# Fused attention and Fourier gate on one core: pair-wise loads of q and k, folded transforms, a new order

## The chip, the core and the metric

The kernel runs on one core of a Trainium2 chip. The metric is the device time of one execution, in microseconds; the lower, the better. The engines are PE (matrix products; PEld is its weight load), DVE (VectorE), ACT (ScalarE), POOL (GpSimd, here mostly the queue that issues casting loads) and SP (SyncE, the queue of the other transfers).

## The reference

Four batches, 8 heads, 768 tokens, head width 64, model width 512. Attention with a window of 96 tokens and 8 global tokens, a linear bias per head, then a gate with a circular convolution over the tokens, done by Fourier transform:

```python
scores = scale * q @ k.T + bias          # bias = -slope[h] * distance, masked outside window and globals
a = softmax(scores); x = a @ v           # x: (B, S, H*D)
x1, x2, x3 = split(x @ w_proj)           # 512 columns each
x2 = irfft(rfft(x2) * rfft(filter))      # over the 768 tokens
out = (x1 * x2 * x3) @ w_out
```

## The kernel before

Everything is 16-bit in SBUF with 32-bit sums. A batch passes two stages; the next batch's attention is interleaved with the present batch's convolution.

**Attention.** k and v are cut into 7 tiles of 120 tokens with the 8 global tokens in front (`GRP` groups the tiles: 0-1, 2-3, 4-6); q into 6 tiles of 128 tokens. `load_q`, `load_run` and `load_rows` load a tile with all 8 heads, k and v over POOL's queue with a cast, q of batch 0 as 32-bit over SP into the output buffers `ot`. `turned` (and `turned32` for batch 0's q) transposes a tile by products with the identity (L640, L627) into `QT` and `KT`. `scores` makes, for a head pair and a group, the products of k and q with 64 rows, two heads side by side (L680). In batch 0 the bias is added by products of `slope` (diagonals) with the distance tile `near`, in two halves of 64 rows (L671), and in the later batches by a product with `mask` on DVE (L711). ACT takes the exponential (L694). `values` (L729, L734) sums with v, which has columns of ones for the denominators; DVE divides (L753); `transpose_x` gives `xT`.

**Gate and convolution.** `gate` makes x1 and x3 (L843) and their product `g`. `butterfly` splits x over the 768 tokens by a factor of 6 on DVE (sums and differences of L788 to L799: `xo`, `xr`, `xcf`). `conv` projects these (L910), `spectra` transforms them by products with the cosine and sine tables `fwd` (L614): two products of 512 columns for each of four outputs, one for each of two. DVE multiplies by the filter's spectrum (`h1`, `h2`; `prod`, `sums`). The inverse (L935, L938) has per bank two products of 256 columns and two of 128. `mixed` and `gated` undo the factor of 6 and multiply by the gate on DVE (L1018 to L1041); the last product with `wo` (L962) is evacuated into `ot` and stored over SP.

**Setup.** `setup`, `load_first`, `distances`, `masks` and `tables` fill constants: ones columns of both v buffers (L1097, L1099), `near`, `slope`, `mask`, the tables (an angle product on PE, rounding on DVE, a sine on ACT; here behind the exponentials of batch 0), then `spectrum` transforms the filter. Before any data is there, PE runs filler products on zeros (L302, the words `i26b1` and the like in the order).

**Order.** The order of all 1025 steps is written out in `ORDER`, with the engine and the PSUM banks of each: `97P01` is step 97 on PE with banks 0 and 1, `98A` step 98 on ACT. Each engine runs its steps in that order; many evacuations may be on ACT or DVE, and the word says which. The steps are numbered as the code makes them.

Of the kernel before, what the change touches and what calls it, by code (L numbers as in the profile page):

```python
# [16 lines left out]
P = 128  # L17
# [3 lines left out]
MAGIC = 12582912.0  # L21
H_SCALE = 1.0 / 32.0
# [17 lines left out]
0V 8V 31V 11V 7V 12V 1V 10V 9V 17S 50S 15S 16S 48S 49S 58S 18G 5G 39A 35A 42A 43A 45A 41A 6A 47A 37A 32A 2A  # L40
38A 36A 33A 46A 51A 19G 22G 23V 28A 40A 44A 26V 55G 24G 71V 72A 77A 34A 79A 52V 25V 61G 54G 59G 60G i26b1 80P0
86P1 87V 81V 29V 259G 20G 21G 57G 67G 56G 62G 3G i2b3 89P2 90V 27V 30V 88V 53V 13V 261S 260G 64G 63G 65G 257G
256G 258G 68G 66G 70G 69G 82P3 83A 84P4 85A 74A i3b1 109P5 110A 75A 115P3 116V i1b0 91P67 92A 93P01 94A 113P2
114V 269G 270G 267G 268G 273G 263G 95P45 96A 78A 161P6 111P7 112V 157P3 158V 162V 14V 97P01 98A 119P45 120A
123P23 124A 121P67 122A 159P0 160V 262S 265S 264S 275G 274G 276G 279G 277G 266G 271G 155P1 156V 104P45 105V
106V 4V 117P23 118A 167P01 168A 165P67 166A 163P45 164A 99P23 100V 101V 215P0 216A 76A 107P1 108V 130P67 131V
132V 125P23 126V 127V 217V 218V 169P45 170A 73A 102P1 103A 220P6 360P7 488G 490S 272G 495G 133P2 134A 219A
221A 128P3 129V 176P45 177V 178V 361V 171P01 172V 150P3 152V 173V 222V 223V 140P2 142A 356P4 357A 179P5 180V
135P7 358P3 359A 224A 137A 174P2 175V 209V 226V 201V 202V 151P4 153A 154V 204V 371P01 365P23 366A 372A 145P5
147V 208V 203V 210V 211V 205V 206V 196P4 227P6 232A 146P7 148A 149V 234V 230V 235V 212V 207V 213V 236V 237V  # L50
225V 373V 214V 136P5 138A 198A 182P2 192P3 194A 368P01 369A 362P45 363A 197P7 199A 191P3 141P0 143A 228A 231A
193A 229A 233A 144V 238V 370V 195V 298P1 285P0 286A 281P7 282A 184A 386P6 387A 299A 498G 499G 294P0 295A 384P7
385V 239V 367V 139V 283P3 284A 186P6 188A 394P45 395A 397P01 398A 430P7 431V 289P2 290V 364V 181P3 309P6 310A
183A 432P7 433V 240V 396V 503G 504G 278G 489G 492G 485G 486G 502G 497G 487G 388P45 389A 391P01 392A 434P2 435V
390V 491S 505G 501G 496G 187P6 189A 296P7 297A 379P45 380V 381V 436P23 437A 374P01 375V 399V 376V 393V 720G
247P6 248A 439P45 440A 441V 438V 307P7 308A 287P2 288A 241P3 442P01 443A 405P45 406V 190V 407V 242V 382P6 383A
243P7 244A 302P2 303A 400P01 401V 402V 377P6 378V 444V 445P45 446A 447V 408P7 245P3 246A 300P2 301A 249P01
251A 409A 250V 403P6 404A 253P45 254A 255A 304V 292V 448P23 449V 450A 185V 453P01 454V 291V 455V 293V 252V
200V 311V 312V 722S 493S 729G 426P7 420P6 421P4 415P5 417A 422A 423A 411P0 413A 410P1 584P5 585A 456P6 457V
305V 660P4 661A 588P0 589V 306V 717G 713G 735G 716G 718S 494S 714G 313P2 314A 317P3 451P5 452A 412A 318A 479V  # L60
478V 425P6 614P2 615A 727G 734G 506G 726G 280G 732G 662P0 719S 721S 464P4 466A 428A 427A 586P1 587V 414V 612P5
613V 481V 480V 725G 508G 724G 658P3 730G 500G 715G 728G 731G 733G 723G 507G 736G 321P2 322A 663A 323P4 324A
327P1 328V 429V 482V 659V 424V 483V 474P7 476A 319P2 320A 469P0 471A 599P45 600A 590P67 591A 325P2 315P1 316A
326A 473P0 475V 484V 329V 330V 331V 522P3 523A 625P45 596P67 597A 598V 622P01 623A 624V 468P2 526P3 527A 470A
626A 509P6 510V 592V 332V 333V 524P7 525A 616P01 593P23 594A 617A 511P6 512V 601V 595V 336V 513P7 514A 664P45
665A 619P23 667P01 668A 620A 458P6 460V 477V 337V 459P7 461A 517P4 416P5 418A 518A 607P01 602P23 603V 608V
419V 604V 609V 621V 618V 334V 666V 335V 627V 515P7 516A 535P5 536A 530P6 531A 350P4 351A 537P5 812P7 813A
353P6 354A 673P23 674A 538A 670P01 671A 463P4 465A 528P7 529A 842P6 843V 628P23 629V 462V 630V 675V 672V 344P5
610P6 611A 345A 816P4 890P7 605P2 606A 817A 633P01 634V 635V 669V 520V 539V 519V 533V 472V 347P6 348A 631P5
886P3 636P2 637A 887A 632A 891A 341P4 676P01 677V 814P6 815A 342A 681P23 682V 540V 678V 532V 683V 467V 534V  # L70
521V 840P5 841A 644P7 888P6 889A 646A 648P4 650A 653P5 655A 679P0 680A 643P1 645V 847P67 848A 821P45 822A
684P2 547P0 548V 685V 823V 706V 849V 707V 649P3 651A 555P6 556A 549P7 550A 853P01 827P45 828A 898P23 899A
545P6 546A 854A 338P7 339V 708V 340S 349S 352S 355S 346S 343S 638P4 640A 551P5 552A 541P2 553P3 554V 709V 710V
711V 543P6 544A 542A 557V 558V 712V 559V 702P7 818P01 819A 850P45 851A 687P6 639P3 641A 689A 642V 900V 820V
560V 652V 561V 564V 754P2 755A 704A 741P4 742A 844P01 845A 846V 829V 824P23 825A 826V 565V 562V 901P67 902A
739P5 740A 737P4 738A 750P0 892P23 895P67 896A 893A 751A 686P1 688A 752P5 692P4 694A 753A 763P2 743P3 765P0
766A 835P67 836V 837V 563V 903V 697P4 654P1 656A 764A 767V 894V 852V 897V 745P0 746A 699A 744A 578P5 758P1
756P2 757A 759A 856P67 857V 647V 855V 696P4 698A 566P3 567A 579A 568S 580S 830P01 831V 832A 858V 768V 747V
691P4 693A 909P23 910V 761V 581P5 582A 861P67 862V 863A 911V 748V 904P01 905V 749V 906V 760V 575P4 701P2 833P3
834V 657V 912P5 859P6 860A 913A 569P7 838P0 839V 762V 703V 864P6 865A 570A 571S 583S 907P1 908A 934V 935V 936V  # L80
937V 695V 938V 939V 940V 773P3 572P5 573A 774A 769P0 781P6 775P1 777P5 783P7 784A 776A 771P2 772A 782A 778A
770A 867P3 872P7 874A 869A 779P2 780A 785V 786V 700V 787V 788V 690V 789V 790V 791V 792V 958P1 954P0 955A 576A
959A 577S 574S 945P5 946A 941P3 942A 915P0 943P2 944A 969P6 970A 956P1 957A 947P7 948A 882P3 949P2 950A 917A
951V 919P4 967P1 968V 952V 971V 953V 972V 962P5 960P2 961A 884A 877P6 871P7 873A 963A 965V 964V 705V 966V 793V
876P2 866P3 868A 879A 870V 881P7 986P5 990P3 973P0 974A 991A 987A 794P6 977P1 978A 979P0 980V 988P3 989A 975P5
976A 883A 981V 875V 885V 982V 929P1 992P3 993A 878A 795A 994V 995V 983V 984V 996V 997V 985V 796S 800P5 801A
797P0 798A 799S 802S 914P7 916A 918V 999V 998V 880V 1001V 1002V 1000V 803P5 804A 805S 925P6 809P7 810A 811S
920P5 922A 931A 806P0 807A 927A 921A 1014V 1012V 923V 1013V 808S 924P5 926A 928V 1006P7 1007A 1008S 930P6 932A
933V 1015V 1009P4 1010A 1011S 1003P5 1004V 1005S 1022P4 1023V 1024S 1016P7 1017V 1018S 1019P6 1020A 1021S
"""  # L90

# [1135 lines left out]
```

## Time and profile before

| | |
|---|---|
| median of 3 runs | 174.79 us (174.55 to 174.84) |
| profiled execution, first to last instruction | 172.9 us (the profile gives no other time of this execution) |
| busy: PE, DVE, ACT, POOL | 166.8, 158.4, 151.9, 75.8 us |
| weight loads | 106.1 us |
| instructions: PE, DVE, ACT, POOL | 1732, 352, 305, 97 |
| moved by DMA | 20.74 MB |
| granted PE clock | 1.000 |

A row of a group of instructions reads: line, engine, operation, out<-in with shapes, count | busy us, mean ns of one | idle time of the engine ahead of them and who ended it. "Busy" is time in which at least one instruction of the engine is in flight; instructions overlap, so the start-to-start distance is shorter than the mean. A row of the chain of waits is start, length, engine, tile, line, count. A row of the table of stretches is the stretch, its length, busy time (instructions) of PE, PEld, DVE, ACT and POOL, granted clock, DMA share and GB/s. Start times are in us from the first instruction.

### The profile page before, as it was taken

Reading aid. Unit: us, or ns where it says so; the run is one execution under the profiler, and the core shown is the slowest. Engines: PE = TensorE matmul, PEld = TensorE weight load, DVE = VectorE, ACT = ScalarE, POOL = GpSimd, SP = SyncE. Lnnn points to the kernel's source line nnn. Section 1 sums busy time; section 2 is a strip of 40 time slices with the busy share of each in tenths; the row PEclk is TensorE's granted clock in tenths of the full one; section 3 lists DMA queues with packets and bytes.
Section 4 is the critical chain, followed back from the end, with each engine's and each line's share of the span. In section 5 each row is a group of like instructions: output and inputs, shape, how many; then the busy total and the mean of one; then the engine's idle time right before and its main releaser. Section 6 shows DMA issues by size and latency. Waiting matters only on the chain.

```text
span 172.9 us, 4486 instructions
## 1 busy us (share of the span) xinstructions
PE 166.8 (96%) x1732; PEld 106.1 (61%) x1732; DVE 158.4 (92%) x352; ACT 151.9 (88%) x305; POOL 75.8 (44%) x97
## 2 busy tenths in 40 slices
PE   7998999999999999999999999999999999999990
PEld 2374988655665668764657867645577755574530
DVE  6869969999999999999999999999989999989970
ACT  2999899999999999999999999999797897678821
POOL 7999998629989964999760000000000000000000
PEclk9999999999999999999999999999999999999999
DMA  4999999999999996999999000720030303003554
GB/s 86 188 198 166 168 171 177 207 184 153 154 161 145 153 148 50 126 147 175 152 151 57 4 0 4 272 91 0 4 121 6 121 2 121 4 0 151 213 205 161
DMA packets 91133, 20.74 MB, mean 120 GB/s; under 512 B 83864, under 2 KB 88040, under 8 KB 91112
## 3 DMA queue, kind: packets, MB, share of 16 engines
q0 software_dynamic: 80912, 12.14, 96.6%
q1 hardware_dynamic: 10200, 8.31, 15.3%
q8 instruction: 13, 0.21, 0.5%
q14 instruction: 8, 0.07, 0.1%
HBM read 25.84 MB, written 6.29 MB: 186 GB/s over the span
## 4 chain that ended last, share of the span: by engine, by line
PE 93%; DVE 4%; issue 0%; ACT 0%; ACTq 0%; DVEq 0%
PE bank L843 25%; PE bank L910 12%; PE bank L962 12%; PE bank L614 6%; PE bank L680 6%; PE bank L640 6%; PE bank L935 5%; PE bank L302 5%; PE bank L729 4%; PE bank L774 4%; PE bank L734 3%; PE bank L671 2%; PE bank L938 1%; DVE KT L306 1%; DVE vn L1097 1%; DVE vn L306 1%
## 5 line engine op out<-in xcount | busy, mean ns | idle before, releaser
L843 PE MATMUL bank<-xT,w 128*128 128x384 f16 x256 | 48.7, 326 | 0.0
L694 ACT ACTIVATE E<-bank 128x864 f16<-128x864 f32 x48 | 40.6, 902 | 1.3 <-PE bank L680 1.3
L843 PEld LDWEIGHTS <-w 128*128 128x128 f16 x256 | 23.4, 98 | 15.6 <-issue 0.7
L322 POOL DMA_DIRECT2D kn<-in_k_dram x28 | 25.7, 921 | 10.7 <-PE bank L640 4.3
L322 POOL DMA_DIRECT2D vn<-in_v_dram x28 | 25.6, 921 | 1.7 <-DMA wo<-in_moe_w_out_dram 1.1
L962 PE MATMUL bank<-wo,y 128*128 128x512 f16 x96 | 23.8, 379 | 0.0
L711 DVE TENSOR_TENSOR E<-E,mask 128x864 f16<-128x864 f16 x36 | 20.6, 600 | 0.0
L322 POOL DMA_DIRECT2D qn<-in_q_dram x18 | 16.3, 918 | 0.3 <-issue 0.2
L753 DVE TENSOR_TENSOR xn<-bank,rc 128x512 f16<-128x512 f32 (+1 forms) x21 | 16.1, 771 | 0.3
L853 ACT CAST g<-bank 128x384 f16<-128x384 f32 x32 | 15.4, 512 | 1.1 <-PE bank L843 0.9
L310 ACT ACTIVATE ot<-bank 128x512 f32<-128x512 f32 x20 | 11.9, 611 | 4.9 <-PE bank L962 4.9
L729 PE MATMUL bank<-vn,E 128*128 128x65 f16 x224 | 15.2, 193 | 0.0
L729 PEld LDWEIGHTS <-E 128*128 128x128 f16 x224 | 14.0, 97 | 1.8
L734 PE MATMUL bank<-vn,E 128*128 128x65 f16 x192 | 14.9, 193 | 0.0
L306 ACT CAST eo<-bank 128x384 f16<-128x384 f32 x28 | 12.7, 512 | 1.7 <-PE bank L938 0.9
L680 PE MATMUL bank<-QT,KT 64*128 64x216 f16 (+2 forms) x224 | 14.0, 241 | 0.0
L306 ACT CAST X<-bank 128x512 f16<-128x512 f32 x22 | 12.7, 613 | 1.3 <-PE bank L614 1.2
L962 PEld LDWEIGHTS <-y 128*128 128x128 f16 x96 | 8.8, 98 | 8.1
L310 ACT ACTIVATE ab<-bank 128x512 f16<-128x512 f32 x22 | 12.8, 619 | 1.1 <-PE bank L910 1.0
L310 ACT ACTIVATE x<-bank 128x384 f16<-128x384 f32 x26 | 13.1, 523 | 0.8 <-ACT g L853 0.4
L734 PEld LDWEIGHTS <-E 128*128 128x128 f16 x192 | 13.1, 97 | 0.7
L680 PEld LDWEIGHTS <-KT 64*128 64x128 f16 x224 | 8.5, 94 | 6.6 <-issue 5.0
(144 smaller groups left out, 369.3 us busy)
## 6 DMA issues: line engine op xcount, KB each, us to landing
out_dram<-ot SPq DMA_DIRECT2D x24, 256.0 KB
kn<-in_k_dram POOLq DMA_DIRECT2D x28, 120.0 KB, 6.3
vn<-in_v_dram POOLq DMA_DIRECT2D x28, 120.0 KB, 6.4
qn<-in_q_dram POOLq DMA_DIRECT2D x18, 128.0 KB, 6.5
ot<-in_q_dram SPq DMA_DIRECT2D x6, 256.0 KB
w<-in_moe_w_proj_dram POOLq DMA_DIRECT2D x4, 256.0 KB, 7.3
g<-in_moe_filter_fft_dram POOLq DMA_DIRECT2D x1, 768.0 KB, 11.0
w<-in_moe_w_proj_dram POOLq DMA_DIRECT2D x1, 512.0 KB, 12.7
```

Source lines behind the costliest of these rows:

```text
L306: {"A": nc.scalar.copy, "V": nc.vector.tensor_copy, "G": nc.gpsimd.tensor_copy}[e](out, in_)
L310: self.nc.scalar.mul(out, in_, c)
L322: return self.g.op(eng, 0.57 + 0.00035 * nbytes[0] if eng == "G" else 0.5, lambda _: e.dma_start(dst, src), w=w, r=r, nbytes=nbytes, name= ...
L680: nc.tensor.matmul(bs[hh].f32()[:, off:off + w], self.KT[hs, hp, P * m:P * m + P], self.QT[hs, hp, KL * m:KL * m + w], start=(off == 0 and ...
L694: g.op("A", act(864), lambda _: nc.scalar.activation(eo, bs[0].two()[:, :, 0:432].rearrange("p h (m w) -> p h m w", m=2), Act.Exp, scale=s ...
L711: g.op("V", dve(864, 2), lambda _: nc.vector.tensor_mul(eo, eo, mk), r=[("mask", 2 * hp), ("mask", 2 * hp + 1)], w=[("E", hp, gi)], name=" ...
L729: nc.tensor.matmul(o[:, n, hh], ef[:, at:at + P], vt[:, t, 2 * hp + hh, 0:D + 1], start=first, stop=(t == 0), skip_group_check=True)
L734: nc.tensor.matmul(o[:, n, hh], ef[:, at:at + P], vt[:, t - 1, 2 * hp + hh, 0:D + 1], start=False, stop=True, skip_group_check=True)
L753: nc.vector.tensor_mul(to, o[:, :, :, 0:D], rc.to_broadcast([P, 2, 2 * nt, D]))
L843: nc.tensor.matmul(bk.f32()[:, 0:h], self.w[:, c, o + P * j:o + P * j + P], self.xT[:, c, h * s:h * s + h], start=(c == 0), stop=(c == 3))
L910: nc.tensor.matmul(bk.f32(), src[:, c], w[:, c, DM:2 * DM], start=(c == 0), stop=(c == 3))
L962: nc.tensor.matmul(bk.f32(), y[:, c, P * t:P * t + P], self.wo[:, c, :], start=(c == 0), stop=(c == 3))
```

## The change

- **q and k by head pair.** `load_pair` loads, for a head pair, all 768 tokens of q and k in six 128-token tiles: two loads for q, two for k, over POOL; for pair 0 of batch 0 over SP as 32-bit into `stage` (the space of `h1`, `h2`) with a cast by DVE or ACT. `turned` makes 6 transposes for a pair's q or k; k's evacuation puts the 120-token tiles and the global tokens together in three pieces. The global rows of k are no longer copied by SP.
- **Tables first.** `tables` moves ahead of the attention and has a third bank of angles (`fold`, half-shifted); the warming ACT function is the sine. The filter's load is at the head of POOL's loads.
- **Biases.** `dg` holds one distance tile with all 128 rows and 648 columns; a block is two products of 128 rows and 432 columns.
- **Folded transforms.** `butterfly` adds and subtracts mirrored halves (`xs`), so that `spectra` needs one product for each of four outputs; `mixed` undoes the fold behind the inverse (`uw`), whose products have 128 columns. Three of these four kinds of adds have an operand or result with a step of minus one.
- **Lighter fills.** The ones are written as pairs in 32-bit words and fewer of them; `kn` needs no zeros; the global rows of v are copied by SP.
- **New order.** 1034 steps, 14 filler products in place of 32, evacuations redistributed; the last batch's last output tile is stored in two halves.

```diff
-        self.qn = t("qn", [P, 6, H, D])
-        self.kn = t("kn", [P, 7, H, D])
+        self.qn = t("qn", [P, 4, 6, 2, D])
+        self.kn = t("kn", [P, 4, 6, 2, D])
...
+    def load_pair(self, b, hp):
+        for i, (what, x, dst) in enumerate((("q", self.q, self.qn), ("k", self.k, self.kn))):
+            to = dst[:, hp]
+            if b or hp not in self.PLAIN:
+                for hh in range(2):
+                    self.load("G", to[:, :, hh], x[b, 2 * hp + hh].rearrange("(t p) d -> p t d", p=P),
+                              [(what + "n", hp, hh)], (768, 256), f"{what}{hp}")
+                continue
...
+            for t in range(6):
+                nc.tensor.transpose(b.f16()[:, P * t:P * t + P], buf[:, hp, t].rearrange("p h d -> p (h d)"), self.ident)
...
+            self.copy(e, kt[:, 0:6, NG:], src[:, 0:6 * KL].rearrange("p (t c) -> p t c", t=6))
+            self.copy(e, kt[:, 6, NG:], src[:, S - KL:S])
+            self.copy(e, kt[:, :, 0:NG], src[:, None, 0:NG].to_broadcast([P, 7, NG]))
...
-                for at, w in runs:
-                    for k in range(2):
-                        for hh in range(2):
-                            hs = slice(64 * hh, 64 * hh + 64)
-                            nc.tensor.matmul(bs[hh].f32()[:, off:off + w], self.slope[hs, hp, k],
-                                             self.near[hs, k, at:at + w], start=(off == 0 and k == 0),
-                                             stop=False, skip_group_check=True)
+                for hh in range(2):
+                    o = bs[hh].f32()[:, 0:432]
+                    nc.tensor.matmul(o if gi != 1 else o.rearrange("p (a b) -> p a b", a=2),
+                                     self.slope[:, 2 * hp + hh], at, start=True, stop=False, skip_group_check=True)
...
+        right, left = cf[:, :, :, 64:P], cf[:, :, :, 63::-1]
+        turned = xs.rearrange("p (a b) c m -> p a b c m", a=2)[:, ::-1, :, :, 64:P]
+        def odd(_):
+            for a in range(2):
+                ins = slice(2 * a, 2 * a + 2)
+                v.tensor_sub(turned[:, a], right[:, ins], left[:, ins])
+        op(dve(512 * n, 2), lambda _: v.tensor_add(xs[:, :, :, 0:64], right, left), ("xr", "xc", "xf"), "xe")
+        op(2 * dve(256 * n, 2), odd, ("xr", "xc", "xf"), "xd")
...
-            self.forward((s,), lambda i, t: self.ab[i][:, t], lambda i, t: [("ab", i, t)], [bk])
+            g.op("P", pe(512), lambda _, bk=bk, i=i, t=t, table=table: nc.tensor.matmul(
+                bk.f32(), table, self.ab[i][:, t], start=True, stop=True), acq=[bk], name="fwd",
+                r=[("ab", i, t), ("fwd", 1 if s > 3 else 3)])
...
-                            nc.tensor.matmul(o[:, 0:P] if z else o[:, P:3 * P], X[:, s, cs],
+                            to = o[:, 0:P] if z else o[:, P:3 * P].rearrange("p (a m) -> p a m", m=64)
+                            to = to if z else to[:, 1:3] if s % 2 else to[:, 0:4:3]
+                            nc.tensor.matmul(to, X[:, s, cs],
                                              self.inr[:, s - 4] if z else self.inv[:, (s + 2) % 4],
...
+        op(lambda _: v.tensor_add(both[:, :, :, 64:P], even, odd), (), "up")
+        op(lambda _: v.tensor_sub(both[:, :, :, 63::-1], even, odd), (), "um")
...
+            self.nc.vector.memset(vt[:, 0, :, self.D:].bitcast(F32), ONES)
+            self.nc.vector.memset(vt[:, 1:, :, self.D:self.D + 2].bitcast(F32), ONES)
...
+        self.load("S", vt[0:NG, 2:7], vt[0:NG, 0:1].to_broadcast([NG, 5, self.H, self.VD]), [("vng", 0, 1)],
+                  (40, 16 * self.VD), "vglobal", r=[("vng", 0, 0, 0), ("vn1", 0)])
```

572 lines of the change are left out of this document (242 added, 330 removed).

## The prediction

> **What bounds the kernel now.** First the busy times and the chain of waits on the page, then the table of stretches.
>
> ```profile
> PE 166.8 (96%) x1732; PEld 106.1 (61%) x1732; DVE 158.4 (92%) x352; ACT 151.9 (88%) x305; POOL 75.8 (44%) x97
> PE 93%; DVE 4%; issue 0%; ACT 0%; ACTq 0%; DVEq 0%
> 0.00:30.00 30.00, 28.32 (x377) 19.31 (x378) 23.75 (x65) 25.37 (x50) 27.83 (x44) 1.00 1.76 165
> 30.00:120.00 90.00, 90.00 (x963) 57.91 (x962) 88.93 (x189) 88.82 (x168) 48.00 (x54) 1.00 1.44 122
> 120.00:165.00 45.00, 45.00 (x380) 27.53 (x379) 42.99 (x97) 36.49 (x88) 0.00 (x0) 1.00 0.19 71
> 165.00:172.90 7.90, 3.46 (x17) 1.37 (x14) 2.68 (x5) 1.20 (x2) 0.00 (x0) 1.00 0.52 200
> ```
>
> Read quickly, this says "PE": 96% busy, 93% of the chain. The stretches (columns after the length: PE, PEld, DVE, ACT, POOL) say more. From 30 to 120 us three engines are full at once: DVE is idle for 1.07 of 90 us, ACT for 1.18. Only from 120 to 165 is PE alone: ACT idles 8.5 us, DVE 2.0. So taking work from PE pays at once in the last third; in the middle, DVE and ACT take its place as the limit. DVE's idle time is 6.25 us up to 30, 3.1 up to 165, and then 0.6 until its last instruction; what follows that is the tail.
>
> Durations overlap, so a sum needs start-to-start distances:
>
> ```profile
> 66.12 0.89 PE bank L640 x16
> 137.39 1.30 PE bank L843 x8
> 138.69 0.27 PE bank L935 x3
> 164.14 4.33 PE bank L962 x20
> 158.38 0.42 DVE L1021 TENSOR_TENSOR eo<-mix,eo 128x512 f16<-128x512 f16 x1
> 158.72 0.42 DVE L1022 TENSOR_TENSOR eo<-mix,eo 128x512 f16<-128x512 f16 x1
> 156.51 1.58 ACT L310 ACTIVATE ot<-bank 128x512 f32<-128x512 f32 x3
> 167.63 0.69 DVE L312 TENSOR_SCALAR ot<-bank 128x512 f32<-128x512 f32 x1 [0.17 <-PE bank L962]
> ```
>
> PE: 0.0556 us for 128 columns, 0.1625 for 384, 0.2165 for 512. The three of L935 are two of 256 and one of 128, so (0.27 - 0.056)/2 = 0.107 for 256. DVE: two of 512 start 0.34 apart and last 0.42, so an instruction that follows directly costs its duration less 0.08. ACT: (1.58 less one duration of about 0.61)/2 = 0.49 for 512. DVE ends at 167.63 + 0.69 = 168.3, 4.6 before the end: that tail (last evacuation and store) I keep, since the new order also ends with a whole 512-column product, evacuation and store.
>
> **What PE loses.**
>
> ```profile
> L935 PE MATMUL bank<-inv,X 128*128 128x256 f16 x64 | 11.3, 273 | 0.0
> L614 PE MATMUL bank<-ab,fwd 128*128 128x512 f16 x40 | 11.3, 379 | 0.0
> L640 PE MATMUL bank<-ident,kn 128*128 128x128 f16 x112 | 8.9, 219 | 0.4 <-DVE KT L306 0.4
> L640 PE MATMUL bank<-ident,qn 128*128 128x128 f16 x72 | 5.7, 219 | 0.0
> 10.63 1.04 PE L627 MATMUL bank<-p,ot 128*128 128x128 f32 x8
> 17.86 0.37 PE bank L671 x8
> ```
>
> Folded inverse: 64 products go from 256 to 128 columns, 64 x 0.051 = -3.3. Folded forward: 40 products become 24 (one, not two, for each of four outputs), 16 x 0.2165 = -3.5. Transposes: 184 at 0.0556 and 24 of 32 bits at (1.04 - 0.27)/7 = 0.11 are 12.9 us; 192 at 0.0556 are 10.7: -2.2. Biases: eight 64-row products of 216 columns take 0.37 a block, since the two halves run side by side; two of 128 rows and 432 columns, between 0.1625 and 0.2165, take 0.36: nothing. The third angle bank adds 0.4. PE in all: -8.6 us.
>
> **What DVE gains and loses.**
>
> ```profile
> L795 DVE TENSOR_TENSOR xo<-xab,xcf 128x1024 f16<-128x1024 f16 x3 | 2.1, 687 | 0.0
> L753 DVE TENSOR_TENSOR xn<-bank,rc 128x512 f16<-128x512 f32 x14 | 9.5, 685 | 0.3
> L1097 DVE MEMSET vn<- 128x1792 f16 x1 | 1.6, 1552 | 0.3 <-issue 0.3
> L306 DVE COPY vn<-vn 8x2560 f16<-8x2560 f16 x1 | 1.5, 1467 | 0.0
> L397 DVE MEMSET kn<- 8x1280 uint32 x1 | 1.1, 1125 | 0.2 <-issue 0.2
> L306 DVE COPY eo<-dg 64x264 bf16<-64x264 bf16 x3 | 1.4, 459 | 0.0
> L306 DVE COPY eo<-dg 64x216 bf16<-64x216 bf16 x3 | 1.1, 352 | 0.1
> L306 DVE CAST eo<-bank 128x384 f16<-128x384 f32 x4 | 2.2, 552 | 0.0
> L306 DVE CAST X<-bank 128x512 f16<-128x512 f32 x2 | 1.4, 682 | 0.0
> ```
>
> Folding moves half of the transform's adds to DVE. With L795 less the overlap, 1024 elements cost 0.61; 512 cost 0.34; so a fixed part of 0.07. Before the transform a batch gets one add of 1024 and two of 512 (1.29 us; batch 0, in halves, 1.5), behind it two of 1024 (1.21; the last batch, in halves, 1.36): 5.4 + 5.0 = +10.4. That holds if a reversed operand keeps the rate; no row shows one. The far bound is L753's one element a cycle: 1024 elements then take 0.61 + 0.53. Three such thousands a batch have a reversed operand, so at most 12 x 0.53 = +6.4 more. I take nothing, since the nearest rows (16-bit, in SBUF, steps of one) are L795's. The Trainium skill, "VectorE: DVE Perf Modes", section "Mode 2×_1P — pack two bf16 into one 32-bit read", asks for 16-bit types and a step of plus or minus one; by that rule too the sum gets nothing, and no run here shows a step of minus one.
>
> Further: two casts of q and k for the first pair, two more rounding steps of the third angle bank, and the constant columns: about +2.5, by L795's and L753's rates. Away go the two memsets of ones (L1097 and its like for the second buffer, 2 x 1.47, for lighter ones that I put at 0.4 each: -2.1), the copy of the global rows (-1.4, to SyncE's queue), the fill of kn (-1.05), the six copies of dg (3 x 0.38 + 3 x 0.27 = -1.95), and about ten small ones that I put at -1.8 together. The order moves casts: counted in the two orders, DVE keeps none of its 4 eo and 2 X and one fewer of ab and x1, and two fewer of ot: 4 x 0.47 + 2 x 0.6 + about 2.3 = -5.4. ACT gets these at about 0.4 to 0.49 each (+4) and loses some slope, near and table-load time, so it stays about level. The evacuations of q and k change shape (21 by DVE before; 10 of 768 and 7 in three pieces after; both 9.4): nothing. DVE in all: +10.4 + 2.5 - 8.3 - 5.4 = -0.8.
>
> So PE gets 8.6 us of air, while DVE keeps 158.4 - 0.8 = 157.6. DVE becomes the bound, and its idle time decides.
>
> **Idle time at the start.**
>
> ```profile
> 29.18 1.30 PE bank L843 x8
> 20.30 0.06 PE bank L729 x2
> L322 POOL DMA_DIRECT2D kn<-in_k_dram x28 | 25.7, 921 | 10.7 <-PE bank L640 4.3 <-PE bank L843 3.2 <-DMA w<-in_moe_w_proj_dram 1.3
> L322 POOL DMA_DIRECT2D g<-in_moe_filter_fft_dram x1 | 0.8, 832 | 0.0
> DMA to landing us min/median/max: 5.2/6.6/12.7
> 17.10 0.56 POOL L380 IOTA X<- 1x512 int32 x1
> 4.23 0.80 POOL L490 TENSOR_SCALAR_AFFINE_SELECT dg<-dg 128x216 bf16<-128x216 bf16 x2
> 1.81 7.44 SPq L322 DMA_DIRECT2D ot<-in_q_dram  x5
> L556 DVE TENSOR_TENSOR pp<-g 128x1536 f16<-128x1536 f16 x2 | 1.9, 945 | 0.0
> 1.20 8.29 PE bank L302 x26
> 6.29 2.70 PEld L302 LDWEIGHTS <-idle 128*128 128x128 f16 x13 [0.28 <-issue]
> ```
>
> Before, values start at 20.3 and the first gates at 29.2. After, a head pair needs all its tokens, and POOL's queue has, ahead of the load of v0, the filter and 12 loads of q and k (13 x 0.83: as many pieces as the filter's row), three of v (0.92 each, v1, v4, v2), and a dozen iotas, selects and fills between 0.2 and 0.56 each (L380, L490: about 4 us). With a start at 1.3 that is 1.3 + 10.8 + 2.8 + 4 = 19; v0 is issued at 20 and lands 6.6 later, at 26.5. SyncE is no obstacle: five q loads of 1024 pieces took it 7.44, so q0 and k0 with 1536 each are issued near 6, and the copy of the global rows behind them lands long before the values that wait for it; nothing but the next batch's copies stands behind it. The last v lands near 29, gates begin at 31 to 34. Until 26.5 DVE has setup, tables, casts, six evacuations and the whole filter spectrum, whose load has been moved to the queue's head (two of L556, four of 1024, smaller ones and two casts: about 6.5): 19 to 20 us of work. So it idles about 6.5 us ahead of the gates, 5 if loads land in 5.2, 9 if the second gate weights hold it (behind v0's issue at 20 three v, two weights and four loads of the next batch, 7.7, and 6.6 to land: 34). That is what it idled before (6.25); the longer start is paid by the spectrum being done in it.
>
> The filler products fall from 32 to 14. The first twelve of L302 are 0.43 apart (1.20 to 6.29), the next thirteen 0.21: PE starts at half rate. In the new start PE waits for data between small groups and may stay at half rate; its 5 us of work before 16 us then take 10 and fit the wait. The granted clock column shows 1.00 throughout, so the spacing alone shows it. The Trainium skill, "TensorE: Matmul & The Clock Gate", section "Part 1: The HAM clock gate (the "warmup" mystery)", says that the clock halves after an idle window of about 3.4 us and needs as long of sustained work to return. By that rule, which speaks against dropping fillers, the sum would get up to 1.7 us more (half of 3.4); the spacing at the start agrees, a later return to half rate no run here shows.
>
> **The sum.** The profiled execution lasts 172.9; the median of the runs, 174.79, lies 1.9 above, which I add. DVE idle ahead of the gates 6.5, DVE work 157.6, idle behind it at the pace of 30 to 120 us (1.07 in 90, so 1.6 in 130; PE is no longer the limit), tail 4.6: 170.3. With 1.9: 172.2, round 172. With DVE idle behind the gates as before (3.7), 174.3; with 5 at the start, 170.7.
>
> **Rivals.**
> - *PE stays the bound.* DVE's waits shrink by as much as PE's work. For it: the chain is 93% PE. Against it: DVE and ACT are 99% busy from 30 to 120. Then 174.8 - 8.6 = 166.2.
> - *Reversed operands run at one element a cycle* (the other side). Place: the two folds of each batch, eight adds around the transforms. +6.4 on an engine that has no more than 1.6 + 2.1 us of air: 172 + 6.4 = 178.4. It decides as soon as more than 2.8 of the 6.4 appear. For it: no row with a reversed step. Against it: the rows of the same type and size all run at two.
> - *The start starves.* q and k loads queue for the second gate weights, and PE adds a cold start: 9 us of idle for 6.5 and the old 3.7 behind, 172 + 2.5 + 2.1 = 176.6 at worst, about 174.8 at half of it.
>
> **How the numbers follow.** Forecast 0.5, PE-bound 0.2, reversed 0.18, starved 0.12. Below 174.44 (0.2%, about what a measurement of this kernel can tell from none) lie 0.9 of the forecast, all of the PE case, and some of the starved: 0.45 + 0.20 + 0.05 = 0.70. Same: 0.07, from the forecast's upper end and the starved start. Slower: 0.18 + 0.05 = 0.23. The range goes from the PE case, 166, to 177.5, which takes in the starved start and a reversed rate that is hit only in part. The forecast's own range is 170.5 to 174.5.
>
> **What would show it.** Right: from 35 to 150 us DVE at 99% and PE visibly below full, 24 forward products of the batches in place of 40, inverse products at 128 columns, the chain passing through DVE; the new adds of 1024 near 690 ns; first gates at 31 to 34. Wrong: reversed adds near 1200 ns; PE full to the end with DVE idle (PE rival); values later than 28 or DVE idle beyond 8 us ahead of the gates (starved).

## The result and the profile after

The changed kernel takes 173.35 us (median of 20 runs, 172.60 to 176.86), the kernel before 174.77 on the same chip (20 runs, 174.21 to 175.71). The ratio is 0.9922, 95% interval 0.9901 to 0.9944: faster by 0.8%, where 1.6% was forecast. The profiled execution takes 172.79 (span 170.9, 1.9 around it), close to the forecast 172.2. The median stands 0.56 above it. In 6 of the 20 runs TensorE's mean clock was 0.988 to 0.990 and the time 174.7 to 176.9, and without these six the median is 173.05: about half of the 0.56 comes from them, the rest from a profiled run that was among the fastest. The ratios here leave out the runs that the low clock disturbed most, the medians hold all.

The page and the table of stretches (same columns as before):

```profile
PE 160.0 (94%) x1617; PEld 96.0 (56%) x1617; DVE 154.8 (91%) x381; ACT 153.2 (90%) x318; POOL 85.5 (50%) x111
PE 54%; POOL 22%; ACT 11%; DMA 7%; issue 3%; DVE 1%; POOLq 0%; ACTq 0%
0.00:30.00 30.00, 25.42 (x277) 13.65 (x278) 23.50 (x87) 25.33 (x45) 28.45 (x45) 1.00 1.63 143
30.00:120.00 90.00, 88.32 (x981) 55.71 (x978) 87.28 (x197) 88.09 (x180) 57.08 (x67) 1.00 1.44 118
120.00:165.00 45.00, 44.29 (x360) 25.92 (x359) 43.12 (x98) 38.82 (x93) 0.00 (x0) 1.00 0.23 89
165.00:170.90 5.90, 1.94 (x10) 0.73 (x8) 0.93 (x2) 0.98 (x2) 0.00 (x0) 0.96 0.47 175
```

The chain of waits, 93% PE's before, now runs for a fifth of the span through POOL's queue and for 7% through DMAs. All three engines lose 1.7 to 2.7 us of the 90 between 30 and 120; most of that is one place (a wait of 1.6 to 1.8 us on each). The waits (columns: total us, times, longest), then the chain around it, TensorE's timeline and SyncE's there:

```profile
PEld L706 <- DMA vn<-vn: 2.1, 1, 2.1
DVE rc L735 <- PE bank L711: 1.9, 2, 1.6
ACT X L305 <- PE bank L1003: 1.8, 1, 1.8
PE bank L706 <- DMA kn<-in_k_dram: 1.6, 1, 1.6
```

```profile
39.61 7.17 DMA w<-in_moe_w_proj_dram
47.06 0.83 POOL qn L321
47.89 4.18 DMA kn<-in_k_dram
```

```profile
50.11 0.38 PE L1003 MATMUL bank<-ab,fold 128*128 128x512 f16 x1
52.08 0.23 PE L706 MATMUL bank<-vn,E 128*128 128x65 f16 x2 [1.60 <-DMA kn<-in_k_dram]
```

```profile
47.67 1.43 SPq L321 DMA_DIRECT2D vn<-vn  x2
```

and SyncE's copies in the kernel before:

```profile
44.09 1.42 SPq L322 DMA_DIRECT2D vn<-vn  x2
```

At 50.5 us TensorE comes to the first value products of batch 1 and waits. The page names a k load; PEld's row and SyncE's timeline say what was late: SyncE's copies of the global rows (vn<-vn) are issued at 47.67, when batch 1's first value load has landed, and that load stood in POOL's queue behind the last weights. Before, the copies were issued 3.6 us earlier, and TensorE came to these products at 51.51 without a wait. The other engines run dry behind TensorE.

### The profile page after: what moved, and what is told of

Same layout as the page of the kernel before. It is cut to its first block, busy times and chain, and to the rows that moved or that the text cites. A ratio compares the mean times of both kernels' runs of the same rounds, so it can differ in the third digit from the quotient of the medians.

```text
span 170.9 us, 4288 instructions
## 1 busy us (share of the span) xinstructions
PE 160.0 (94%) x1617; PEld 96.0 (56%) x1617; DVE 154.8 (91%) x381; ACT 153.2 (90%) x318; POOL 85.5 (50%) x111
## 4 chain that ended last, share of the span: by engine, by line
PE 54%; POOL 22%; ACT 11%; DMA 7%; issue 3%; DVE 1%; POOLq 0%; ACTq 0%
PE bank L829 16%; PE bank L943 12%; PE bank L887 8%; POOL kn L321 7%; POOL qn L321 7%; ACT E L671 4%; DMA w<-in_moe_w_proj_dram 4%; POOL vn L321 4%; PE bank L751 3%; PE bank L706 3%; PE bank L911 3%; PE bank L1003 3%; DMA kn<-in_k_dram 2%; PE bank L711 2%; PE bank L626 2%
## 5 line engine op out<-in xcount | busy, mean ns | idle before, releaser
L671 ACT ACTIVATE E<-bank 128x864 f16<-128x864 f32 x48 | 43.1, 957 | 0.7 <-PE bank L660 0.6
L321 POOL DMA_DIRECT2D qn<-in_q_dram x30 | 26.8, 918 | 0.7 <-DMA w<-in_moe_w_proj_dram 0.4
L321 POOL DMA_DIRECT2D kn<-in_k_dram x30 | 26.7, 910 | 0.0
L943 PE MATMUL bank<-wo,y 128*128 128x512 f16 (+1 forms) x100 | 23.7, 370 | 0.7 <-DVE y L992 0.7
L309 ACT ACTIVATE ot<-bank 128x512 f32<-128x512 f32 (+1 forms) x23 | 14.2, 631 | 5.1 <-PE bank L943 4.4
L839 ACT CAST g<-bank 128x384 f16<-128x384 f32 x32 | 16.6, 561 | 1.1 <-PE bank L829 1.1
L305 ACT CAST X<-bank 128x512 f16<-128x512 f32 x24 | 15.6, 704 | 1.8 <-PE bank L1003 1.8
L887 PE MATMUL bank<-w,xs 128*128 128x512 f16 x64 | 15.5, 379 | 0.0
L305 ACT CAST eo<-bank 128x384 f16<-128x384 f32 x32 | 15.1, 590 | 0.0
L309 ACT ACTIVATE x<-bank 128x384 f16<-128x384 f32 x27 | 14.9, 580 | 0.0
L711 PEld LDWEIGHTS <-E 128*128 128x128 f16 x192 | 13.2, 97 | 0.8 <-issue 0.2
```

What stands on the lines that cost most here:

```text
L305: {"A": nc.scalar.copy, "V": nc.vector.tensor_copy, "G": nc.gpsimd.tensor_copy}[e](out, in_)
L309: self.nc.scalar.mul(out, in_, c)
L321: return self.g.op(eng, 0.57 + 0.00035 * nbytes[0] if eng == "G" else 0.5, lambda _: e.dma_start(dst, src), w=w, r=r, nbytes=nbytes, name= ...
L671: g.op("A", act(864), lambda _: nc.scalar.activation(eo, bs[0].two()[:, :, 0:432].rearrange("p h (m w) -> p h m w", m=2), Act.Exp, scale=s ...
L711: nc.tensor.matmul(o[:, n, hh], ef[:, at:at + P], vt[:, t - 1, 2 * hp + hh, 0:D + 1], start=False, stop=True, skip_group_check=True)
L839: g.op("A", act(h), lambda _: nc.scalar.copy(x3, pts[1].f32()[:, 0:h]), use=[pts[1]], w=[ko], name="x3")
```

## The experiments

Two marks are read from each trace: where batch 1's first value products begin, and how long the span still lasts. Each mark is that of one execution; the ratio, over several, is to the kernel before, run alongside.

| kernel | begin | from there | ratio to before (95%) |
|---|---|---|---|
| before | 51.51 | 121.4 | 1 |
| changed | 52.08 | 118.8 | 0.9922 (0.9901–0.9944) |
| more fillers | 53.34 | 118.8 | 0.9939 (0.9914–0.9963) |
| before, fewer fillers | 51.40 | 121.4 | 1.0009 (0.9989–1.0029) |
| values later | 52.73 | 118.6 | 0.9921 (0.9892–0.9950) |
| scale in table | 53.09 | 117.9 | 0.9883 (0.9836–0.9930) |
| less DVE | 52.56 | 118.8 | 0.9883 (0.9842–0.9924) |
| less PE | 52.72 | 118.3 | 0.9873 (0.9849–0.9896) |
| less ACT | 52.37 | 119.2 | 0.9907 (0.9874–0.9941) |
| unfolded | 52.75 | 123.8 | 1.0167 (1.0136–1.0197) |
| pair 1 by SyncE | 57.62 | 118.5 | 1.0157 (1.0117–1.0197) |
| pairs 1, 2 by SyncE | 65.42 | 118.4 | 1.0652 (1.0598–1.0705) |
| scale and tail | 51.80 | 117.8 | 0.9843 (0.9821–0.9865) |
| fewer loads | 50.14 | 118.8 | 0.9817 (0.9789–0.9844) |
| value load earlier | 50.39 | 118.8 | 0.9874 (0.9853–0.9894) |
| all three | 50.51 | 118.9 | 0.9833 (0.9798–0.9867) |

(Texts written before the runs count the second mark to the start of the last product: 4.3 to 4.4 us less.) The traces of less ab, less exp, all three cuts in one and the folded kernel before (119.8, 120.3, 121.4 and 136.1 from the mark) hold windows at half rate behind the mark, see below, and aren't in the table.

### Fillers

```diff
-... 20V 62A 86P3 ... 49G i2b6 88P0 ... 55G i5b6 ... 47A i5b0 100P2
+... 20V 62A i3b6 86P3 ... 49G i3b6 88P0 ... 55G i6b6 ... 47A i8b0 100P2
```

> The changed kernel with 22 filler products in place of 14, so that TensorE has no idle time from 1.2 to 14.4 us. Theory A (the median of the changed kernel, 173.35, stands 0.5 above its profiled execution because in about a third of its runs TensorE falls back to half rate for one more window, and it does so after the waits of 0.5 to 1.2 us in its first 15 us): the median falls to about 172.8 and every run shows a granted clock of 0.995 or more. Rival (the runs of 175 to 177 us come from the wait of all engines at 50 us, not from the start): the clock of 0.988 to 0.990 still appears in about a quarter of the runs, median 173.0 to 173.6. Rival (fillers only delay the tables): slower by up to 1 us.

Measured 174.08 (12 runs), clock 0.989 to 0.990 in three of them. TensorE was now busy for 12.71 of the 13.2 us from 1.2 to 14.4 (10.26 in the changed kernel), and the lower clocks stayed: theory A falls.

```diff
-... 60G i26b1 80P0
+... 60G i8b1 80P0
```

> The kernel before with 18 fewer filler products (the first group 8 in place of 26; 14 in all, as many as the changed kernel has). Theory A: some of its runs now show a clock of 0.988 to 0.990 and a time 2 to 3 us longer, and its median rises by 0.2 to 1 us from 174.8. If the fillers don't matter, median 174.5 to 174.9 and all clocks at 0.995 or more. If the fillers are in the way of the transposes behind them, it is faster, 174.0.

174.60 (12 runs, 174.35 to 175.98), ratio 1.0009 (0.9989 to 1.0029): in the kernel before, 18 of the fillers at the start are worth nothing that these runs can tell. In the profiled run the mean clock was 0.994 at 174.58 us, as full rate ended at 170.6 us, behind the last product. Three other runs had 0.987 to 0.990 and took 174.35 to 174.76; only the one with 0.975 was longer, 175.98. A mean clock says little until one looks where it fell.

### Moving the value products, and the scales

```diff
-277P0 374P23 433A ... 392V 375V 278A ... 290P0 276A
+277P0 433A ... 392V 278A ... 290P0 374P23 276A 491G 375V
```

> The changed kernel with the first value products of batch 1, which wait 1.60 us at 50.4 us for the copy of the global rows, moved behind one projection, one score block and two forward products (1.6 us of TensorE's work); VectorE's reciprocal is moved with them. Theory B (what stops all three engines at 50 us is lost for good, since they are full behind it): 1.0 to 1.6 us faster than the changed kernel, 171.9 to 172.4 at its median. Rival (the next load in POOL's queue, or the full queues of ScalarE and VectorE, end the same wait a little later): within 0.3 us, 173.0 to 173.6.

173.18 (7 runs): the rival. 1.6 us of TensorE's work now lies ahead of the wait, and it comes back behind it: from the value products on, the span shrinks by 0.2 only. What follows seems tied to these products, not to TensorE's load.

```diff
+ for s in range(4): fold[:, (s+2)%4] *= part[:, s]    # behind the transposes
- (xs, ..., self.part[:, 2*i:2*i+1])
+ (xs, ..., 1.0)
```

> The changed kernel with the per-partition scales of the ab evacuations (16 of 24) multiplied into the forward table once, behind the transposes that make the inverse tables; the evacuations then have a constant scale. From the trace of the changed kernel ScalarE's pitch falls from 0.578 to 0.490 us in 15 of them: -1.3 us of ScalarE's time, +0.4 on VectorE. Theory C (ScalarE is as much the limit as VectorE): 0.5 to 1.0 us faster than the changed kernel, about 172.6. Theory D (VectorE alone is the limit, as the prediction has it): nothing or 0.4 slower, 173.4 to 173.8.

All runs: 173.53 (6, two with a clock of 0.99); ratio 0.9883, 0.7 us less than the changed kernel's, with intervals that overlap. In the groups of the changed kernel, then of this one,

```profile
L309 ACT ACTIVATE ab<-bank,part 128x512 f16<-128x512 f32 x15 | 11.0, 801 | 0.2 <-PE bank L887 0.2
```

```profile
L309 ACT ACTIVATE ab<-bank 128x512 f16<-128x512 f32 x23 | 14.6, 676 | 1.4 <-PE bank L893 1.4
```

the evacuation with a scale per partition lasts 801 ns, the same with a constant 676 (ends in a full queue lie 0.578 and 0.490 us apart in the changed kernel's trace, which has both kinds). The Trainium skill, "ScalarE: Activation LUTs", section "What ACT_TABLE_LOAD costs", puts a pointer operand at about 93 ns; the 88 ns between the ends agree. The prediction had not priced this part of the change. The second mark falls by 0.9 us for 1.3 of ScalarE's time (15 x 0.088).

### Five microseconds off one engine, and off all

```diff
-nc.vector.tensor_mul(eo, eo, mk)
+part, mk = (eo[:, 0], mk[:, 0]) if gi < 2 else (eo, mk)
+nc.vector.tensor_mul(part, part, mk)
```

> The changed kernel, but 24 of the 36 mask products of batches 1 to 3 are done for one head of the pair only (432 elements in place of 864; the other head's scores stay unmasked): 24 x 0.225 = 5.4 us less on VectorE, nothing else touched. Theory D (VectorE alone is the limit, as the prediction has it): 4 to 5 us faster than the changed kernel, 168.5 to 169.5. Theory C (VectorE, ScalarE and TensorE stand within a few us of each other and each holds the others up through their queues): 0.5 to 1.5 us faster, 172 to 173.

```diff
-for c in range(4):
+for c in range(4 if o else 3):
```

> The changed kernel, but the first product of each gate sums three of its four parts: 32 x 0.1625 = 5.2 us less on TensorE, nothing else touched. Theory D: nothing, 173.0 to 173.6, since TensorE has 10.9 us of idle time already. Theory C: 0.5 to 2 us faster, most of it behind 120 us, where TensorE is full for 44.3 of 45 us.

```diff
-nc.scalar.copy(x3, pts[1].f32()[:, 0:h])
+nc.scalar.copy(x3h, pts[1].f32()[:, 0:h // 2])
```

> The changed kernel, but the 32 copies of the gates' second product out of PSUM take half of their 384 columns (the product with the first one reads the half twice): 32 x 192/1.2 per ns, about 5.1 us less on ScalarE, VectorE and TensorE unchanged. Theory D: nothing, 173.0 to 173.6. Theory C: 0.5 to 2 us faster. If ScalarE is the engine that sets the pace between 30 and 120 us, 3 us or more.

Medians 174.10, 172.79, 173.42 (4 runs each); second mark 118.8, 118.3, 119.2 against 118.8. By the ratios the three are 0.7, 0.9 and 0.3 us faster than the changed kernel, and only the interval of less PE lies clear of it. Theory D falls: 5.4 us less on VectorE give nothing behind 52 us. Its waits from 53 to 120 us in that kernel show where they went:

```profile
DVE rc L736 <- PE bank L712: 3.0, 4, 1.9
DVE uw L968 <- ACT eo L305: 0.9, 1, 0.9
DVE pp L1025 <- ACT X L305: 0.6, 1, 0.6
```

In the changed kernel the same list holds one wait of 0.2. What VectorE gains it gives back at the next result of another engine. TensorE does too, but its busy time hardly shows it: behind the mark less PE has 26 products of 0.1625 us fewer, 4.2 us, and TensorE's busy time (the first figure behind the length) falls by 1.0 in these stretches of the changed kernel, then of less PE:

```profile
53.00:120.00 67.00, 66.92 (x774) 43.07 (x772) 66.39 (x143) 66.23 (x138) 34.50 (x41) 1.00 1.22 100
120.00:160.00 40.00, 39.99 (x335) 23.61 (x334) 39.29 (x88) 36.06 (x88) 0.00 (x0) 1.00 0.23 86
```

```profile
53.00:120.00 67.00, 66.40 (x765) 42.05 (x762) 66.03 (x143) 65.59 (x137) 34.39 (x40) 1.00 1.21 100
120.00:160.00 40.00, 39.56 (x327) 22.75 (x326) 39.47 (x88) 36.62 (x89) 0.00 (x0) 1.00 0.23 86
```

A product of 384 columns lasts 0.33 us and the next one starts 0.16 behind it, so a wait shorter than the overlap is counted as busy.

The three edits in one kernel:

> The changed kernel with the three cuts of the runs before made together (mask products of 24 of 36 for one head only, first gate product without its fourth part, second gate product half copied): about 5 us less on each of VectorE, TensorE and ScalarE. Each cut alone gave nothing (the distance from the first value products of batch 1, 52 us, to the last product was 114.5, 114.0 and 114.9 us, against 114.5). Theory C (the three engines hold each other up, so a cut of one is given back at its next wait on another): together 3 to 5 us faster, 168 to 170, and that distance 110 to 112. Rival E (something else sets the pace behind 52 us, the loads or a chain of latencies): again under 1 us, 172.3 to 173.5.

172.17 (5 runs), 0.9845 (0.9822 to 0.9868): 1.2 us by the medians, 1.3 by the ratios, for all three cuts. That is more than rival E allows and far less than theory C asks.

```diff
-self.times(e, self.ab[i][:, t, :], bk.f32(), k)
+self.times(e, self.ab[i][:, t, 0:n], bk.f32()[:, 0:n], k)    # n = 256 if b else 512
```

> The changed kernel, but the 18 evacuations between projection and forward transform of batches 1 to 3 take 256 of 512 columns: 18 x 0.21 = 3.8 us less on ScalarE. Theory F (behind 52 us the pace is set by a chain of hand-offs between TensorE and ScalarE in the written order, on which these evacuations stand and the gates' copies do not): 1.5 to 3 us faster than the changed kernel, 170 to 171.5. If ScalarE's load counts no more here than it did for the gates' copies (5.1 us less gave nothing): 172.6 to 173.6.

```diff
-eo, bs[0].two()[:, :, 0:432]...(m=2), Act.Exp
+eo[:, :, :, 0:n], bs[0].two()[:, :, 0:432]...(m=2)[:, :, :, 0:n], Act.Exp    # n = 144 if b else 216
```

> The changed kernel, but the 36 exponentials of batches 1 to 3 take 144 of 216 columns of each tile: 36 x 0.24 = 8.6 us less on ScalarE, its largest group. Theory F: if the exponentials stand on the chain, 3 to 6 us faster, 167 to 170. If not: under 1 us.

173.04 (10 runs), 0.9891 (0.9870 to 0.9912); 172.21 (4 runs), 0.9857 (0.9827 to 0.9887). By the ratios 3.8 us off ScalarE give 0.5, 8.6 give 1.1: both below what theory F asks, so it falls in this form. That shortening the ab evacuations by 1.3 us in all (the scales) took 0.9 off the second mark does show that they stand on the chain, for a part of a microsecond. So no cut of one engine's load brings much behind 52 us; that the order of hand-offs between the engines sets the pace there is argued, not shown, and stays open.

### The folds

```diff
-xs = right + left, right - left; uw = even + odd, even - odd
+matmul(bk, fold[:, s], ab[i][:, t], start=False)    # a second forward product, s < 4
-matmul(to, X, inv[:, (s + 2) % 4])
+matmul(o[:, P:3 * P], X, inv[:, at:at + 2])
```

> The changed kernel with the folding of both transforms priced backwards: the reversed sums and differences ahead of the forward and behind the inverse transform are left out (VectorE -10.4 us by the prediction's working), the 16 odd forward products are made twice and the 64 inverse products take 256 columns (TensorE +6.8). The output means nothing; only the load on the engines is that of unfolded transforms. If the prediction's account holds (folding buys 6.8 us of TensorE for 10.4 of VectorE, and TensorE was the bound): 0.5 to 2 us slower than the changed kernel, 174 to 175. If VectorE's load is what limits the changed kernel, folding is no gain: 171.5 to 173.

177.67 (4 runs), 1.0167: folding is worth 4.3 us in this order, more than the whole change brings. In numbers of the table, 123.8 against 118.8 behind 52 us. So more work on TensorE counts for the most part (6.8 us more, 5.0 longer, though VectorE had less to do), while 5.2 us less gave 0.5: TensorE stands near its limit there, and another limit lies just below. VectorE then works 12.0 us less between 30 and 165 us (118.4 for 130.4), and TensorE fills the last third:

```profile
30.00:120.00 90.00, 88.02 (x954) 55.31 (x951) 79.32 (x174) 85.98 (x175) 57.23 (x67) 1.00 1.45 117
120.00:165.00 45.00, 45.00 (x370) 27.26 (x369) 39.08 (x85) 39.52 (x94) 0.00 (x0) 1.00 0.20 77
```

The reverse of that edit, on the kernel before:

> The kernel before with the folding of both transforms alone, priced and not computed: the reversed sums and differences are added on VectorE at both transforms (+10.4 us by the prediction's working, 5.1 in the stretch where VectorE idled 1 us of 90), forward products are halved in number (-3.5) and inverse products take 128 columns (-3.3). Loads, tables, biases and order are those of before. If the fold pays by itself and the rest of the change (the new start) eats 2.9 of its 4.3 us: 170.5 to 172. If the fold only pays with the new order, since VectorE and ScalarE are full in the old one: 174 to 178.

194.4 (4 runs), 1.1086 (1.1004 to 1.1169): worse than either guess. In the old order projections stand right behind the last sums, and TensorE waits for the folded ones (the granted clock falls behind such waits, to 0.953 in the mean):

```profile
ACT ab L311 <- PE bank L920: 22.0, 8, 5.3
PE bank L920 <- DVE xs L809: 13.3, 5, 4.5
```

In the old order the fold doesn't pay; it needs another, and the changed kernel's is one.

### The loads

```diff
-PLAIN = (0,)
+PLAIN = (0, 1)          # and (0, 1, 2); 50G 51G 52G 49G become 49S 51S, 50V 52V
```

> The changed kernel with the second head pair of batch 0 loaded as the first one is: by SyncE as 32-bit, with a cast on VectorE (2 x 0.66 us), so that four loads of 0.83 us leave POOL's queue ahead of the values. Theory P (POOL's queue paces the first 52 us: its loads follow each other without a gap, and everything behind the first value products of batch 1 runs at a fixed pace): values of batch 0 begin at 22 in place of 25.2, the first projection at 43.6 in place of 46.9, and the whole is 2 to 3 us faster, 170.3 to 171.3. Rival (VectorE, ScalarE and TensorE set the pace from 30 us on, whatever lands earlier): values earlier, first projection within 1 us of 46.9, the whole within 0.7 us of 173.0.

> As the run before it, with the third head pair too: eight loads leave POOL's queue, four casts (2.6 us) come to VectorE. Theory P: 6.6 us less queue; SyncE's issues (two or more us for each of these loads, by the trace of the kernel before) and the casts become the limit of the start, so 2 to 4 us faster than the changed kernel, 169 to 171. Rival: within 0.7 us of the run before it, or slower by the casts.

177.34 and 186.14: both expectations missed. The loads that SyncE issues at 2.41 land 11.6 us later, and VectorE, in order, stands at their cast (timeline of the first kernel):

```profile
2.41 1.66 SPq L323 DMA_DIRECT2D g<-in_q_dram  x1
14.00 0.56 DVE L307 CAST qn<-g 128x768 f16<-128x768 f32 x1 [4.50 <-DMA g<-in_q_dram]
```

TensorE also ran at half rate (clock 0.50) from 18.07 to 24.89 us in the first kernel and from 16.25 to 33.31 in the second. So theory P isn't tested by them; but they show that a start 5 to 13 us longer moves everything and leaves the second mark at 118.4 to 118.5.

```diff
 for hh in range(2):
+    if b == 1 and hh: continue
     self.load("G", to[:, :, hh], ...)
```

> The changed kernel without the loads of the second head of each pair of q and k of batch 1 (8 of the 57 loads that POOL issues before 47 us; the heads keep batch 0's data): 6.6 us less of POOL's queue and 6144 fewer pieces. Theory G (loads, by POOL's issue or by the DMA engines behind it, set when the middle columns of the weights and the values of batch 1 are there, and with them the 52 us at which the fixed stretch of 114.4 us begins): first projection at 41 to 44 in place of 46.9, first value products of batch 1 at 48 to 50.5 in place of 52.1, the whole 1.5 to 3.5 us faster. Rival (the engines need these 52 us themselves): projection earlier, but the whole within 0.7 us of 173.0.

171.50 (4 runs), 0.9817 (0.9789 to 0.9844). The last weights are issued at 33.48 (39.61), and the first projection still comes at 46.75 (46.93): between the first values (25.18 and 25.23, behind loads that are the same in both) and the projection these loads don't set the pace. The wait at 50 us is gone, and the span is 2.0 shorter. So theory G is right about the time and the value products, wrong about the projection.

```diff
-75G ... 182P3 258G ... 76G 150A 365P67 259G 212V
+75G ... 182P3 259G 258G ... 76G 150A 365P67 212V
```

> The changed kernel with one line of the order changed: batch 1's first value load stands ahead of the last four q and k loads in POOL's queue in place of behind the last weights (4.3 us earlier; those five loads 0.93 later). Theory H (the fixed stretch of 114.4 us begins when the first value products of batch 1 begin, these wait for the copies of the global rows and so for this load, and a wait of over 2 us there brings TensorE's clock down for 3.4 us more): first value products at 50.2 to 50.9 in place of 52.1, no wait there of over 1 us, the whole 1.0 to 1.9 us faster than the changed kernel, 171.1 to 172.2, and fewer runs above 174. Rival (the last q and k loads or the weights, now 0.93 later, stop TensorE in its place): within 0.5 us of 173.0.

172.28 (5 runs, 171.19 to 173.64), 0.9874 (0.9853 to 0.9894): by the ratios 0.8 us faster than the changed kernel, by moving one load. SyncE's copies and the products they release, in this kernel:

```profile
41.82 1.43 SPq L321 DMA_DIRECT2D vn<-vn  x2
50.39 0.23 PE L706 MATMUL bank<-vn,E 128*128 128x65 f16 x2
```

SyncE's first line lies 5.9 us earlier and no wait is left. Theory H holds in its mechanism; the gain of 0.8 is a little less than the 1.0 that it asked for. (The profiled run, the fastest of the five, is 1.7 shorter than that of the changed kernel.)

### Put together

```diff
-919P6 931V 802S ... 1020V 916V 933V    # and the scales in the table
+919P6 931A 802S ... 1020V 916A 933V
```

> The changed kernel with the scales in the forward table (the run before that did this alone stood at 0.9883 of the kernel before, against 0.9922 for the changed kernel), and with two of the last gates' first evacuations moved from VectorE to ScalarE: they stand on VectorE (0.55 us each) between the last sums and the product for which TensorE waits 0.70 us at 163.5 us, while ScalarE idles there. Expected: the wait of 0.70 goes, 1.0 to 1.6 us faster than the changed kernel, 171.4 to 172.0. If the products behind them are held by the projection of the same half anyway: 0.6 to 0.9 (the scales alone).

171.77 (5 runs), 0.9843: that looks like the scales alone, since the second mark is that of the run with the scales (117.8 and 117.9). TensorE still waits 0.8 us in the tail.

```diff
-394A 271P5 287V 274A 277P0 374P23    # and the scales, the tail, the value load
+394A 374P23 271P5 287V 274A 277P0
```

> Everything that helped in one kernel: the scales in the forward table, the two evacuations of the tail on ScalarE, batch 1's first value load ahead of the last q and k loads, and its first value products two places earlier in TensorE's order. Theory H: the products begin at 49 to 50, and the gains add up: 2.5 to 4 us faster than the changed kernel, 169 to 170.5. If the products now wait for their exponentials or the weights: 170.8 to 171.8, as the run with the first two edits.

171.54 (6 runs, 170.63 to 172.64), 0.9833: faster than the changed kernel, but the gains don't add up: it lies level with the kernel with the first two edits. (Its value products stand two places earlier, so its second mark isn't to be compared.) The first projection comes at 48.19 for 46.93, with 0.4 us of waiting for the weights, which are one load later.

### When the clock falls

Some traces show the half rate in the middle of the run. Stretches cut at the steps of the recorded clock, which come in windows of 3.41 us, first of the kernel with less ab, then of that with less on all engines, then of that with less PE:

```profile
49.57:52.98 3.41, 0.85 (x7) 0.25 (x6) 1.44 (x3) 2.24 (x5) 3.41 (x5) 1.00 2.33 168
52.98:56.39 3.41, 3.41 (x24) 1.49 (x24) 2.07 (x5) 0.56 (x1) 3.41 (x5) 0.50 2.36 152
```

```profile
92.46:95.87 3.41, 1.29 (x16) 0.98 (x17) 1.02 (x4) 1.69 (x9) 0.00 (x0) 1.00 0.45 33
95.87:99.28 3.41, 3.41 (x34) 2.87 (x32) 3.41 (x5) 2.14 (x5) 0.00 (x0) 0.50 0.00 0
```

```profile
48.75:52.16 3.41, 1.49 (x7) 0.49 (x5) 2.30 (x6) 2.98 (x6) 3.41 (x5) 1.00 2.31 167
52.16:55.57 3.41, 2.85 (x42) 1.74 (x43) 2.20 (x6) 1.16 (x3) 3.07 (x4) 1.00 2.46 149
```

The wait at 50 us was 2.56 us long in the first, 2.5 in the third. Where it left TensorE busy for 0.85 of the 3.41, the next window ran at half rate; with 1.49 it did not. So one wait costs itself or itself and up to 1.7 us more (an estimate, half of 3.41), by how it lies on the grid: full rate began at 8.9 to 12.0 us in the kernels with the change. That this is what the six runs of the changed kernel had is argued from its 1.60 us wait and their clock (half of 3.41 in 172 is 0.99); there is no trace of such a run of that very kernel. For it: the two kernels made to remove the wait (fewer loads, value load earlier) show no clock below 0.995 in nine runs. Against it: of the kernels with a wait of 0.2 us (scale and tail) and none (all three), one run in five had 0.990 (175.41) and one in six 0.991 (172.64).

## Why the prediction was right and wrong

- **PE loses 8.6.** The products are as worked out: inverse products of 128 columns, 24 forward products of the batches, no biases of 64 rows. The busy time can't confirm the size: it fell by 6.8, but 4.7 of that are the fillers (the first two lines, before and after), which the 8.6 doesn't hold, and short waits count as busy.

```profile
L302 PE MATMUL bank<-idle 128*128 128x512 f16 x32 | 10.1, 473 | 1.2 <-DVE idle L375 1.2
L301 PE MATMUL bank<-uw 128*128 128x512 f16 x14 | 5.4, 517 | 1.2 <-DVE uw L374 1.2
L911 PE MATMUL bank<-inv,X 128*128 128x128 f16 x64 | 7.9, 219 | 0.0
L1003 PE MATMUL bank<-ab,fold 128*128 128x512 f16 x16 | 5.9, 379 | 0.0
L1003 PE MATMUL bank<-ab,fwd 128*128 128x512 f16 x8 | 3.0, 378 | 0.0
L772 DVE TENSOR_TENSOR xo<-xab,xcf 128x1024 f16<-128x1024 f16 x3 | 2.0, 683 | 0.0
L785 DVE TENSOR_TENSOR xs<-xcf 128x1024 f16<-128x1024 f16 x3 | 2.0, 683 | 0.0
L968 DVE TENSOR_TENSOR uw<-eo 128x1024 f16<-128x1024 f16 x3 | 2.0, 683 | 0.0
```

- **Reversed operands.** Right to take nothing for them, and that rival is dead: reversed (L785 input, L968 output) and unreversed (L772) all last 683 ns. The rule of the Trainium skill, "VectorE: DVE Perf Modes", section "Mode 2×_1P — pack two bf16 into one 32-bit read", holds here for a step of minus one.
- **DVE idle ahead of the gates, 6.5.** Right: 30 - 23.50 = 6.50 up to 30 us; values at 25.2 for 26.5, gates at 32.9 within 31 to 34. The rival of the starved start didn't come true there; a wait for a load came later, at 50 us.
- **DVE idle behind them, 1.6, by the pace of before, "PE is no longer the limit".** The term of the sum that failed: 2.72 + 1.88 up to 165 us and 0.9 more before its last instruction, 5.5 in all. Of the 3.9 too little, 1.6 are the one wait at 50 us. The prediction costed the queue up to the gates and stopped there; batch 1's value load, its copies and who waits for them were not followed. Most of the rest lies behind 120 us: there DVE idled 1.88 of 45 us, nearly as before (2.01), with TensorE still full, 44.29 of 45, and then the 0.9:

```profile
166.11 0.69 DVE L311 TENSOR_SCALAR ot<-bank 128x512 f32<-128x512 f32 x1 [0.88 <-PE bank L943]
```

- **DVE work, 157.6, and the tail, 4.6.** They are 154.8 and 4.1; these 3.3 made up for most of the 3.9 above (which part of the work was put too high stays open). That the profiled span came out at 170.9, so close to 170.3, is luck: errors of over 3 us cancel.
- **DVE becomes the bound.** The step that failed: 5.4 us off it gave nothing behind 52 us. Two of the prediction's own signs failed with it: the chain passes through DVE for 1% only, and PE isn't visibly below full (66.92 of 67 us from 53 to 120). The sum "idle + work + tail" of one engine gave the right span without that engine being the limit.
- **The median 1.9 above the profiled span.** 1.9 holds for the profiled run; the median lies another 0.56 higher, about 0.3 of it by the runs with the low clock. So the median missed 172.2 by 1.15, half in the span, half here. The prediction had the falling clock, and its price, up to 1.7 us, but for the start, where more fillers or fewer made no difference. Two traces of close variants (less ab, less exp) show it behind the wait at 50 us. By the rule of the Trainium skill, "TensorE: Matmul & The Clock Gate", section "Part 1: The HAM clock gate (the "warmup" mystery)", a window of 3.4 us that runs freely decides, and an idle one halves the clock. The traces agree with the window (3.41 us, begun at another point in each kernel), not with idle: 1.29 us of work in it did not hold the clock, 1.49 did.
- **PE stays the bound (166.2).** Wrong in the time, 173.35, and half right in the mechanism: the unfolded kernel says that TensorE stands near its limit (6.8 us more, 5.0 longer), but 5.2 us less on PE gave only 0.5 behind 52 us, so something else does too.

## What to carry to other kernels

When three engines are full, don't look for the one that binds; measure how long the run lasts from a mark on, and which edits move that length. Follow every load that a change moves to its last consumer, through the copies that depend on it; here one load five places earlier in a queue was worth 0.8 us, over half of what the whole change brought. A wait of some 2 us on TensorE can cost up to 1.7 us more than its length, and only in some runs, so a wider spread of times may be a sign of such a wait. And a busy time of 99% doesn't say that work taken away comes back as time, or that it doesn't: short waits hide in overlapping instructions.

## What was not expected of the hardware

In these traces the clock falls by a grid: windows of 3.41 us, half rate for the next one where TensorE was busy for 0.85 to 1.44 us, none where it was for 1.49 or more (the 1.44 from the folded kernel before, 86.20 to 89.61 us). And in the run with less on all engines TensorE stopped amid a group of value products, waiting for nothing that the profile shows,

```profile
94.58 0.20 PE L708 MATMUL bank<-vn,E 128*128 128x65 f16 x1 [2.27 <-issue]
```

while that trace has no transfer on the instruction queue between 70.0 and 92.1 us, where the changed kernel's has one at 84.1. That its instructions came late is a guess from this, not shown: the kernel with less PE has no such transfer between 70.8 and 91.0 us either, and no such stop. The clock fell behind the stop too.
